# Gate angles by arc tangent and running sums, one score product a head, and a checked fallback, in a GateLoop and SwiGLU kernel

## The chip, the cores and the metric

The kernel runs on one core of a Trainium2 chip. The metric is the device time of one execution in microseconds; less is better. The core has a matrix engine (PE, with its weight loads shown apart as PEld), a vector engine (DVE), a scalar engine for activation functions (ACT), a general engine (POOL) and a queue that issues transfers (SP). Each engine takes its instructions in the order of its own queue and waits for others by semaphores.

## The reference

Four batches, eight heads, 768 steps, 48 features a head. A recurrence with complex gates, then a normalised SwiGLU feed-forward over 3,072 tokens:

```python
mag = np.sqrt(a_re * a_re + a_im * a_im)
scale = np.minimum(mag, 0.999) / (mag + 1e-06)
a_re_n, a_im_n = (a_re * scale, a_im * scale)
for t in range(S):
    new_re = ar * S_re - ai * S_im          # ar, ai: gates of step t, one for each feature d
    new_im = ar * S_im + ai * S_re
    S_re, S_im = (new_re + einsum('bhd,bhe->bhde', k[:, :, t], v[:, :, t]), new_im)
    y[:, :, t] = einsum('bhd,bhde->bhe', q[:, :, t], S_re)
x = y as (3072, 384)
xn = x / sqrt(mean(x * x) + 1e-06) * rms_g
g = xn @ w_gate                              # 384 -> 1536
out = (g * sigmoid(g) * (xn @ w_val)) @ w_out
```

The inputs: real parts of the gates are uniform between 0.85 and 0.95, imaginary parts normal with a deviation of 0.1; q, k, v normal with 0.1. The feed-forward's weights arrive as numbers of eight bytes and are made float32 on the chip. All arithmetic is float32.

## The kernel before

A gate is a magnitude times a unit phasor. The product of the phasors since the sequence's first step rotates q and k (each feature gets two rows, cosine and sine, so 96 rows a head), after which the gates are real numbers between 0 and 1. The recurrence then runs in 24 chunks of 128 steps (six for each batch), all heads together.

`gates(b, j, t)` treats 128 feature rows of a batch over all 768 steps, three times for each batch. It computes magnitudes and unit phasors (squares and a square root on ACT, a reciprocal and a Newton step on DVE, lines 103 to 126), then the running product of the phasors by `cmul` over strides 1, 4, 16, 64, 256 and back (lines 151 to 159), six DVE operations for each complex product. Cosines, sines and magnitudes go to DRAM (lines 127 and 161) and come back in the layout of the chunks in `load_unit` (lines 271 and 272).

`levels(n)` computes the weights of all pairs of steps in a chunk, without any quotient. It multiplies q and k by cosines and sines, forms the diagonal by small 32-wide products (line 295), and then goes through seven levels of halves 1, 2, ..., 64. Each level is a set of small matrix products (line 310 inside 32-step blocks, line 322 above), a masked copy or a copy into `am`, and three DVE multiplications that extend the decay factors in q, in k and in the blocks' whole products (lines 327 to 330). So one level waits for the last one's DVE work.

`finish(n)` transposes k (line 350), computes the new state (lines 354 to 361), the outputs y from `am` and v and from q and the carried state (lines 366 and 368), normalises them (ACT squares with an accumulated sum, POOL a power, ACT a scaling), transposes them on PE and scales them into `xT` (line 386).

`feed_forward(g, ffn)` runs for each group of three chunks: twelve steps f of six matrix products each (gate and val, three each; a float32 product shows as two records) with a sigmoid on ACT and two products on DVE (lines 403 to 405), then three outputs of twelve products each (line 410).

`load_weights` and `narrow` load the weights in 18 pieces of 128x768 and convert them with nine DVE operations each.

The order: the phasors of batch 0 first (lines 420 to 425), then for each chunk `step(levels(n), behind, *ahead)`, which advances the levels of the chunk, the finish of the chunk before and the phasors of the next batch in turns, with one step of the filler (weights first, then the feed-forward of the last whole group) after each round. The framework keeps priorities in that order, but puts a ready instruction into an engine's queue ahead of one that isn't expected to be ready. All transfers are issued from SP.

Of the kernel before, what the change touches and what calls it, by code (L numbers as in the profile page):

```python
"""GateLoop (a gated linear recurrence with complex gates) and then a SwiGLU feed-forward, in float32.

The recurrence S_t = a_t S_{t-1} + k_t v_t^T, y_t = q_t . Re S_t runs in chunks of 128 steps.
A gate is a magnitude times a unit phasor. The product of the phasors since the sequence's first
step rotates q and k (two rows of each feature: cosine and sine), after which the gates are real
numbers in [0, 1]. Within a chunk the weights of the pairs (t, s) with s < t come in levels of
halves 1, 2, ..., 64: a pair belongs to the one level where s lies in the lower and t in the upper
half of the same block, and its decay is (product from the upper half's start to t) times (product
after s to the lower half's end). Both are products of gates alone, without a quotient or a
logarithm, so that any gate, zero too, is treated exactly. A level is one set of matrix products  # L10
and the factors of the next level are this level's times the halves' whole products. After the
last level they are what the carried state needs.
"""
# [8 lines left out]
FP32 = mybir.dt.float32  # L22
I32 = mybir.dt.int32
U32 = mybir.dt.uint32
# [5 lines left out]
P = 128  # L30
C = 128          # steps in a chunk
BLK = 32         # steps in a diagonal block
# [3 lines left out]
SCALE = 2.0 ** 30    # gates are scaled by a power of two before they are squared  # L36
TINY = 2.0 ** -112   # squares of scaled gates below this: the gate's own value is 0 in float32
# [3 lines left out]
def gateloop_swiglu(  # L41
    ctx: ExitStack,
    tc: tile.TileContext,
    qT: bass.AP,      # [B * NCH, D, H * C]
    kT: bass.AP,      # [B * NCH, D, H * C]
    v: bass.AP,       # [B * S, H * D]
    a_re: bass.AP,    # [B, H * D, S]
    a_im: bass.AP,    # [B, H * D, S]
# [4 lines left out]
    out: bass.AP,     # [B * S, H * D]  # L53
# [12 lines left out]
    GC = 3               # chunks in a group of the feed-forward  # L66
# [12 lines left out]
    # ---------------------------------------------------------------- phasors and magnitudes  # L79
# [9 lines left out]
    def gates(b, j, t):  # L89
        """Rows j*128.. of batch b: cosine and sine of the phase up to each step, and magnitudes."""  # L90
# [18 lines left out]
        # 1 / m and 1 / (m + eps) from one reciprocal  # L109
# [5 lines left out]
        # one Newton step of r = w ** -0.5  # L115
# [4 lines left out]
        # the unit phasor (1 where the gate is 0)  # L120
# [3 lines left out]
        # min(|a|, cap) * |a| / (|a| + eps)  # L124
# [5 lines left out]
        def cmul(x, y, n):  # L130
            """y *= x for complex views (re, im) of n elements."""
# [13 lines left out]
        def view(step, g):  # L145
            """Every step-th element, in groups of g: [p, groups, g]."""
            n = S // step
            return [q.rearrange("p (n k) -> p n k", k=step)[:, :, step - 1]
                     .rearrange("p (a g) -> p a g", g=g) for q in (re, im)]
# [16 lines left out]
    # ---------------------------------------------------------------- constants  # L166
# [7 lines left out]
    # pairs of a level inside a diagonal block: steps s on the partitions, the block's upper-half  # L174
    # steps t along a row
# [15 lines left out]
    # weights of pairs, [s, head, t]: the parts before a diagonal block stay 0  # L191
# [12 lines left out]
    def load_weights(stage):  # L204
        """Weights of 4 bytes as they are; of 8 bytes, their words (low, high) made float32 here."""
# [298 lines left out]
```

## Time and profile before

| | us |
|---|---|
| median of three runs | 1414.46 (1412.72 to 1414.88) |
| span of the profiled execution | 1409.9 |
| PE busy | 997.1 (71%) |
| PEld busy | 702.6 (50%) |
| DVE busy | 1072.7 (76%) |
| ACT busy | 225.6 (16%) |
| POOL busy | 34.1 (2%) |
| mean granted PE clock | 0.896 |

A profile page describes one execution. "Busy" counts the time in which an engine has an instruction running; matmuls overlap in the pipeline, so the mean duration of one is longer than what it adds to a run of them. The granted clock is the share of full speed at which the throttle lets PE run. A line of a group gives the source line, the engine, the operation, what it writes and reads, the shape and the count, then busy time, the mean in ns of one, and the idle time of the engine just before, with who ended it. A row of a timeline gives start and duration in us.

The page's slices of the span (40, in tenths) show the stages at a glance: PE is at 0 in the first six slices while DVE is at 8 or 9, and in the last four DVE falls off while PE is full.

```profile
PE   0000005245399869986999699869997999799898
DVE  7999998998988978897899798978955642543120
```

### The profile page before, as it was taken

How to read it: one execution, taken by the hardware profiler on the slowest of the kernel's cores; microseconds unless marked ns; L12 is line 12 of the kernel's file. 1: busy time of each engine (PE TensorE's matmuls, PEld its weight loads, DVE VectorE, ACT ScalarE, POOL GpSimd, SP SyncE). 2: the span in 40 equal slices, each digit the busy share in tenths (PEclk: the TensorE clock that was granted, in tenths of full speed). 3: DMA queues.
4: the chain of work that ended last, by engine and by line, in shares of the span. 5: the costliest groups of instructions: out<-in, count | busy, mean ns of one | idle time of the engine just before them, and what ended most of it. 6: DMA issues, size and time to landing. Idle time of an engine off the chain costs nothing.

```text
span 1409.9 us, 30973 instructions
## 1 busy us (share of the span) xinstructions
PE 997.1 (71%) x13352; PEld 702.6 (50%) x13352; DVE 1072.7 (76%) x2663; ACT 225.6 (16%) x453; POOL 34.1 (2%) x54
## 2 busy tenths in 40 slices
PE   0000005245399869986999699869997999799898
PEld 0000005235266555655665666556656667666555
DVE  7999998998988978897899798978955642543120
ACT  1000001111032211211222113112111211111110
POOL 2000000000100000000000000000000000000000
PEclk9999999999999958995899599958995997699899
DMA  6223242241022222302222313021213021100000
GB/s 173 69 99 106 84 119 63 74 136 45 24 75 62 85 62 53 97 29 52 74 57 85 82 39 96 31 73 30 63 63 80 24 52 40 30 1 7 12 1 17
DMA packets 63993, 86.94 MB, mean 62 GB/s; under 512 B 5488, under 2 KB 48496, under 8 KB 63856
## 3 DMA queue, kind: packets, MB, share of 16 engines
q1 hardware_dynamic: 63856, 84.96, 21.5%
q8 instruction: 105, 1.72, 0.5%
q14 instruction: 32, 0.26, 0.1%
HBM read 66.06 MB, written 18.87 MB: 60 GB/s over the span
## 4 chain that ended last, share of the span: by engine, by line
PE 51%; DVE 39%; issue 6%; ACT 1%; DMA 1%; POOL 1%; SPq 0%; POOLq 0%; DVEq 0%; ACTq 0%
PE gate_ps L400 13%; PE val_ps L400 11%; PE out_ps L410 6%; PE s_high L322 5%; DVE k L282 4%; PE s_low L310 4%; PE y_ps L366 4%; DVE w L98 3%; DVE cs L282 3%; PE state_ps L354 3%; PE y_ps L368 3%; DVE re L98 3%; DVE mg L111 2%; DVE s L98 2%; DVE m L98 2%
## 5 line engine op out<-in xcount | busy, mean ns | idle before, releaser
L400 PE MATMUL gate_ps<-xT,wg 128*128 128x384 f32 x576 | 231.7, 539 | 0.7 <-DVE xT L386 0.7
L400 PE MATMUL val_ps<-xT,wv 128*128 128x384 f32 x576 | 205.2, 492 | 0.0
L410 PE MATMUL out_ps<-wo,hT 128*128 128x384 f32 x576 | 192.0, 490 | 0.0
L295 PE MATMUL s_diag<-q,k 96*32 96x32 f32 x1536 | 23.4, 228 | 218.2 <-DVE k L282 214.4
L310 PE MATMUL s_low<-cs,k 96*32 96x16 f32 x7680 | 111.0, 199 | 86.0 <-DVE k L282 77.0
L310 PEld LDWEIGHTS s_low<-cs,k 96*32 96x32 f32 x7680 | 97.8, 131 | 131.2 <-issue 65.8
L400 PEld LDWEIGHTS val_ps<-xT,wv 128*128 128x128 f32 x576 | 110.9, 194 | 79.7 <-issue 5.7
L400 PEld LDWEIGHTS gate_ps<-xT,wg 128*128 128x128 f32 x576 | 113.1, 209 | 64.5 <-issue 13.8
L410 PEld LDWEIGHTS out_ps<-wo,hT 128*128 128x128 f32 x576 | 107.7, 190 | 71.3
L282 DVE TENSOR_TENSOR cs<-cs,bp 96x512 f32<-96x512 f32 x144 | 98.6, 685 | 49.9 <-PE s_high L322 49.7
L295 PEld LDWEIGHTS s_diag<-q,k 96*32 96x32 f32 x1536 | 20.4, 140 | 223.5 <-DVE k L282 214.4
L322 PE MATMUL s_high<-cs,k 96*32 96x32 f32 (+1 forms) x1152 | 79.2, 237 | 68.8 <-DVE k L282 47.4
L322 PEld LDWEIGHTS s_high<-cs,k 96*32 96x32 f32 (+1 forms) x1152 | 70.1, 150 | 88.7 <-issue 70.0
L404 DVE TENSOR_TENSOR sg<-gate_ps,sg 128x384 f32<-128x384 f32 x96 | 52.8, 550 | 63.7 <-ACT sg L403 63.4
L282 DVE TENSOR_TENSOR k<-k,bp 96x512 f32<-96x512 f32 x144 | 97.8, 679 | 0.0
L403 ACT ACTIVATE sg<-gate_ps 128x384 f32<-128x384 f32 x96 | 47.0, 489 | 276.2 <-PE gate_ps L400 263.0
L366 PE MATMUL y_ps<-v,amat 128*128 128x48 f32 x384 | 89.2, 334 | 0.7 <-ACT amat L324 0.7
L368 PE MATMUL y_ps<-state,cs 96*128 96x48 f32 x320 | 80.0, 340 | 0.0
L366 PEld LDWEIGHTS y_ps<-v,amat 128*128 128x128 f32 x384 | 75.2, 249 | 2.4 <-ACT amat L324 0.8
L405 DVE TENSOR_TENSOR hT<-val_ps,sg 128x384 f32<-128x384 f32 x96 | 53.1, 553 | 29.7 <-PE val_ps L400 29.6
L313 DVE COPY_PREDICATED dg<-pairs,s_low 128x128 f32<-128x128 int32 x120 | 41.3, 344 | 43.6 <-PE s_low L310 41.9
L368 PEld LDWEIGHTS y_ps<-state,cs 96*128 96x128 f32 x320 | 66.8, 258 | 0.0
(82 smaller groups left out, 1316.1 us busy)
## 6 DMA issues: line engine op xcount, KB each, us to landing
q<-in_q_dram SPq DMA_DIRECT2D x48, 192.0 KB, 3.4
k<-in_k_dram SPq DMA_DIRECT2D x48, 192.0 KB, 3.6
mg<-mag SPq DMA_DIRECT2D x48, 192.0 KB, 4.1
re<-in_a_re_dram SPq DMA_DIRECT2D x12, 384.0 KB, 3.2
im<-in_a_im_dram SPq DMA_DIRECT2D x12, 384.0 KB, 4.0
v<-in_v_dram SPq DMA_DIRECT2D x24, 192.0 KB, 2.6
raw<-in_w_gate_dram SPq DMA_DIRECT2D x6, 768.0 KB, 4.8
mag<-mg SPq DMA_DIRECT2D x12, 384.0 KB, 2.5
```

What stands on the lines that cost most here:

```text
L98: nc.vector.tensor_tensor(out=o, in0=x, in1=y, op=op)
L282: tt = lambda o, x, y: nc.vector.tensor_tensor(out=o, in0=x, in1=y, op=ALU.mult)
L295: nc.tensor.matmul(ps[bs, h], lhsT=k[:, h, bs], rhs=q[:, h, bs], start=True, stop=True)
L310: nc.tensor.matmul(ps[bs, h].rearrange("s (j r) -> s j r", r=m), lhsT=k[:, h, bs], rhs=rhs, start=True, stop=True)
L322: nc.tensor.matmul(ps[lo, h], lhsT=k[:, h, lo], rhs=qd[:, h, hi], start=True, stop=True)
L366: nc.tensor.matmul(ps[:, h], lhsT=am[:, h], rhs=vv[:, h], start=True, stop=prev is None)
L368: nc.tensor.matmul(ps[:, h], lhsT=qd[:, h], rhs=prev[:, h], start=False, stop=True)
L400: nc.tensor.matmul(p_, lhsT=w_[:, d, fs], rhs=xT[:, d], start=d == 0, stop=d == ND - 1)
L403: nc.scalar.activation(out=sg, in_=gp, func=AF.Sigmoid)
L404: nc.vector.tensor_tensor(out=sg, in0=gp, in1=sg, op=ALU.mult)
L405: nc.vector.tensor_tensor(out=hT[:, f], in0=vp, in1=sg, op=ALU.mult)
L410: nc.tensor.matmul(ps, lhsT=hT[:, f, i * C:(i + 1) * C], rhs=wo[:, f], start=f == 0, stop=f == NF - 1)
```

## The change

The old kernel function stays, renamed `general`, with its comments removed. A new function `fast` computes the same result in another way, and a new `gateloop_swiglu` calls `fast`, reads a flag that `fast` left and runs `general` behind it, in a conditional block, if the flag is above 0.

In `fast`:

- The gates are treated in units of two chunks (12 units), in a layout of 128 rows by 3 x 256 for all heads of the batch. The angle is the arc tangent of im / re; the running angle is a sum (a scan), reduced to one turn by rounding, and its cosine and sine come from the sine function. The magnitude's running product within a chunk is a scan too. q is multiplied by that product and k by its reciprocal, so that one plain matrix product for each head gives all the pairs' weights of a chunk; a causal mask finishes them.
- Rotated q and k are rearranged by transfers inside SBUF from the gates' layout to the 96-row layout; DRAM is no longer passed. The decay over a chunk goes the same way in four-byte rows.
- The state is computed as (state products + old state) x decay.
- ACT's Silu takes the place of the sigmoid and one DVE product.
- Conversion of the weights takes one ACT square and six DVE operations a piece, and the pieces are pulled by the first group's feed-forward, two before every second f.
- Each output of the feed-forward has a second pause in its middle, so a group has 18 filler steps; the loop runs one filler step after each part of the scores and two after each part of the finish.
- The flag counts entries outside the range in which the shortcuts hold: decays of a chunk not between 2^-40 and 1, or real parts outside 2^-7 to 2^7.

The core of the diff (lines of `general` that only lost comments are left out):

```diff
+PI = 3.14159265358979
+ROUND = 1.5 * 2.0 ** 23
+RE_MIN = 2.0 ** -7
+RE_MAX = 2.0 ** 7
+P_MIN = 2.0 ** -40
...
-def gateloop_swiglu(
+def general(
...
+def fast(tc, ctx, qT, kT, v, a_re, a_im, w_gate, w_val, w_out, rms_g, out, H, bad):
...
+    def load_gates(u):
+        b, c = divmod(u * UC, NCH)
+        t = UN[u]
+        for name, ap in (("re", a_re), ("im", a_im)):
+            t[name] = prep.tile([P, ND, T], FP32, tag=name, name=name, bufs=2)
+            rows = ap[b].rearrange("(h j l) s -> j l h s", j=ND, l=L)
+            for j in range(ND):
+                nc.sync.dma_start(out=t[name][:, j], in_=rows[j][:, :, c * C:c * C + T])
...
+    def gates(u):
+        t = UN[u]
+        re, im, q, k = (t[x] for x in ("re", "im", "q", "k"))
+        act_ = nc.scalar.activation
+
+        s, w, y, r, p, ks, qs = (prep.tile([P, ND, T], FP32, tag=x, name=x)
+                                 for x in ("s", "w", "y", "r", "p", "ks", "qs"))
+        act_(out=s, in_=re, func=AF.Square)
+        act_(out=w, in_=im, func=AF.Square)
+        tt(s, s, w, ALU.add)
+        act_(out=y, in_=re, func=AF.Abs_reciprocal_sqrt)
+        act_(out=y, in_=y, func=AF.Square)
+        act_(out=r, in_=s, func=AF.Abs_reciprocal_sqrt)
+        act_(out=w, in_=re, func=AF.Abs, bias=mid)
+        act_(out=w, in_=w, func=AF.Relu, bias=width, accum_out=range_[:, u:u + 1])
+
+        tt(im, im, y)
+        tt(re, re, y)
+        stt(im, re, 2.0, im, ALU.subtract, reverse0=True)
+        yield
+
+        tt(w, s, r)
+        stt(s, w, -0.5, r, ALU.mult)
+        stt(w, s, 1.5, w, ALU.add)
+
+        act_(out=r, in_=r, func=AF.Identity, scale=-CAP * EPS_MAG, bias=cap)
+        stt(w, w, EPS_MAG, r, ALU.subtract, ALU.min)
...
+        nc.vector.tensor_tensor_scan(out=flat(p), data0=flat(w),
+                                     data1=starts.rearrange("p j c t -> p (j c t)"),
+                                     initial=0.0, op0=ALU.mult, op1=ALU.add)
+        nc.vector.tensor_copy(out=ends[:, u], in_=p.rearrange("p j (c t) -> p j c t", t=C)[:, :, :, C - 1])
+        yield
+        act_(out=r, in_=p, func=AF.Abs_reciprocal_sqrt)
+        act_(out=r, in_=r, func=AF.Square)
+        act_(out=im, in_=im, func=AF.Arctan)
+        act_(out=im, in_=im, func=AF.Copy, scale=0.5 / PI)
+
+        tt(s, p, r)
+        stt(r, s, 2.0, r, ALU.subtract, reverse0=True)
+        tt(k, k, r)
+        tt(q, q, p)
+        yield
+
+        for j in range(ND):
+            nc.vector.tensor_tensor_scan(
+                out=re[:, j], data0=im[:, j], data1=zeros, op0=ALU.add, op1=ALU.add,
+                initial=UN[u - 1]["turn"][:, j] if u * UC % NCH else 0.0)
+        act_(out=w, in_=re, func=AF.Identity, bias=round_)
+        stt(im, w, ROUND, re, ALU.subtract, ALU.add, reverse0=True)
+        turn = t["turn"] = prep.tile([P, ND, 1], FP32, tag="turn", name="turn", bufs=2)
+        nc.vector.tensor_copy(out=turn, in_=im[:, :, T - 1:T])
+        act_(out=w, in_=im, func=AF.Abs)
+        act_(out=s, in_=im, func=AF.Sin, scale=2 * PI)
+        act_(out=y, in_=w, func=AF.Sin, scale=-2 * PI, bias=halfpi)
+        yield
+        tt(ks, k, s)
+        tt(k, k, y)
+        tt(qs, q, s)
+        tt(q, q, y)
+        rot = {"kc": k, "ks": ks, "qc": q, "qs": qs}
+        yield
+        for i in range(UC):
+            n = u * UC + i
+            for name in ("k", "q"):
+                to = U[n][name] = unit.tile([D2, H, C], FP32, tag=name, name=name, bufs=3)
+                for a, part in enumerate("cs"):
+                    for j in range(ND):
+                        nc.sync.dma_start(
+                            out=to[a * D + j * L:a * D + (j + 1) * L],
+                            in_=rot[name + part][:, j, i * C:(i + 1) * C])
...
+        nc.scalar.activation(out=to, in_=as_to(hi.bitcast(FP32)), func=AF.Square)
+        stt(as_to(g.bitcast(FP32)), to, (1.125 * 2.0 ** -15) ** 2, as_to(hi.bitcast(FP32)), ALU.is_ge)
...
+    def scores(n):
...
+        for a in range(2):
+            ps = ps_a.tile([C, hh, C], FP32, tag="a", name="s_ps")
+            for h in range(hh):
+                nc.tensor.matmul(ps[:, h], lhsT=k[:, a * hh + h], rhs=q[:, a * hh + h],
+                                 start=True, stop=True)
+            nc.vector.tensor_tensor(out=am[:, a * hh:(a + 1) * hh], in0=ps, op=ALU.mult,
+                                    in1=causal.unsqueeze(1).to_broadcast([C, hh, C]))
+        yield
...
+    def feed_forward(g, pieces):
...
+            if f * P % FW == 0:
+                next(pieces, None)
+                next(pieces, None)
...
+            nc.scalar.activation(out=sg, in_=gp, func=AF.Silu)
+            tt(hT[:, f], vp, sg)
+            yield
...
+                if f == NF // 2:
+                    yield
...
+    load_gates(1)
+    for _ in gates(0):
+        pass
...
+    def run(x, fill):
+        for _ in x:
+            for _ in range(fill):
+                next(filler, None)
+            next(ahead, None)
+
+    behind = None
+    for n in range(N + 1):
+        if n % UC == 0 and n // UC + 1 < NU:
+            for _ in ahead:
+                pass
+            if n // UC + 2 < NU:
+                load_gates(n // UC + 2)
+            ahead = gates(n // UC + 1)
...
+        if n < N:
+            run(scores(n), 1)
+        if n > 0:
+            run(finish(n - 1), 2)
+        if n % GC == 0 and n:
+            for _ in filler:
+                pass
+            filler = feed_forward(n // GC - 1, pieces)
...
+def gateloop_swiglu(tc, qT, kT, v, a_re, a_im, w_gate, w_val, w_out, rms_g, out, H):
+    nc = tc.nc
+    with tc.tile_pool(name="flag", bufs=1) as flag:
+        bad = flag.tile([1, 1], I32, name="bad")
+        with ExitStack() as ctx:
+            fast(tc, ctx, qT, kT, v, a_re, a_im, w_gate, w_val, w_out, rms_g, out, H, bad)
+        with tc.If(nc.values_load(bad[0:1, 0:1]) > 0):
+            general(tc, qT, kT, v, a_re, a_im, w_gate, w_val, w_out, rms_g, out, H)
```

216 lines of the change are left out of this document (added).

## The prediction

> **What bounds the kernel now.** I read the page's chain of work first, then the waits, then a cut of the span into stretches. In the page's part 4 (share of the span by engine) and in the view of the waits (total, times, longest) these lines carry it; the four rows of the windows view give a stretch, its length, then the busy time of PE, of weight load (PEld), of DVE, ACT, POOL with counts, the granted clock and the DMA share:
>
> ```profile
> PE 51%; DVE 39%; issue 6%; ACT 1%; DMA 1%; POOL 1%; SPq 0%; POOLq 0%; DVEq 0%; ACTq 0%
> PE s_diag L295 <- DVE k L282: 214.4, 1, 214.4
> 0.00:214.00 214.00, 0.00 (x0) 0.00 (x0) 206.13 (x510) 12.36 (x14) 9.54 (x30) 1.00 0.36 108
> 214.00:391.00 177.00, 78.27 (x2034) 72.16 (x2034) 163.90 (x414) 22.18 (x49) 10.44 (x3) 1.00 0.25 70
> 391.00:1334.00 943.00, 847.29 (x11105) 588.65 (x11104) 688.77 (x1715) 183.69 (x376) 14.14 (x21) 0.85 0.20 54
> 1334.00:1410.00 76.00, 71.53 (x217) 41.76 (x216) 13.93 (x25) 7.32 (x15) 0.00 (x0) 0.97 0.02 8
> ```
>
> There are four stages with different limits. For 214 us PE has no record at all: DVE computes the phasors of batch 0 in 206 us of its time, and the first score product waits for it. To 391 us DVE is still 93% busy (164 of 177) and PE 44%. Then PE and DVE take turns as the bound, at a mean granted clock of 0.85. The last 76 us are the feed-forward of the last group, PE alone.
>
> **What PE's work costs.** A matmul's shown duration contains its latency, so I take start-to-start distances in the timeline (start, duration), where PE runs without a gap at full clock:
>
> ```profile
> 1340.23 2.10 PE L400 MATMUL gate_ps<-xT,wg 128*128 128x384 f32 x6
> 1342.16 2.10 PE L400 MATMUL val_ps<-xT,wv 128*128 128x384 f32 x6
> 1344.10 2.10 PE L400 MATMUL gate_ps<-xT,wg 128*128 128x384 f32 x6
> 1382.80 23.38 PE L410 MATMUL out_ps<-wo,hT 128*128 128x384 f32 x72
> 824.65 0.55 PE L385 MATMUL xT_ps<-ident,xn 128*128 128x128 f32 x3
> 825.03 2.10 PE L400 MATMUL gate_ps<-xT,wg 128*128 128x384 f32 x6
> 859.57 0.88 PE L350 MATMUL kt_ps<-ident,k 96*128 96x96 f32 x8
> 860.38 0.36 PE L310 MATMUL s_low<-cs,k 96*32 96x16 f32 x18
> 860.69 1.56 PE L354 MATMUL state_ps<-v,kt 128*96 128x48 f32 x16
> 862.09 2.17 PE L400 MATMUL gate_ps<-xT,wg 128*128 128x384 f32 x6
> 866.63 0.42 PE L366 MATMUL y_ps<-v,amat 128*128 128x48 f32 x2
> ...
> 870.28 2.25 PE L400 MATMUL gate_ps<-xT,wg 128*128 128x384 f32 x3
> ```
>
> One f of the feed-forward is 1344.10 - 1340.23 = 3.87 us, so 12 are 46.4; the three outputs are about 23.3. A group is **69.7 us**, eight are 558. The change leaves these products alone. Of a chunk, kt is 0.81, state 1.40, y 3.65 and xT 0.38 us; these stay too. kt, state and half of y are missing in one chunk of six, or so little fewer that I take 5.5 us a chunk for them together.
>
> **The change, term by term.**
>
> *Scores.* The levels go (64 s_diag, 320 s_low and 48 s_high records a chunk, with the DVE work between them). In their place stand 8 heads x 2 records with 128 weight columns and 128 moving ones. The trace has no such pair in float32. y, 32 records in 3.65 us, has 128 weight columns and 48 moving ones: 0.114 us each, set by the weights. If the 128 moving columns (384 take 3.87 / 12 = 0.32, so 0.107) lie beside the load, a chunk costs 16 x 0.114 = 1.8 us; if behind it, 16 x 0.22 = 3.5. I take 1.9, since y shows loads beside the stream. So attention is **7.4 us a chunk**.
>
> *The clock.* Low-stream work drops the clock:
>
> ```profile
> 684.00:732.00 48.00, 48.00 (x552) 30.91 (x551) 43.38 (x87) 12.06 (x24) 0.55 (x1) 1.00 0.14 39
> 732.00:744.00 12.00, 12.00 (x160) 8.62 (x159) 9.95 (x74) 1.83 (x5) 0.55 (x1) 0.86 0.21 50
> 744.00:774.00 30.00, 30.00 (x279) 17.74 (x279) 29.93 (x49) 6.66 (x11) 0.00 (x0) 1.00 0.28 94
> ```
>
> PE is busy throughout and still gets 0.86 in the 12 us with a y: 1.7 us lost. In the new order state and y stand together (5 us of narrow products), so I take 2.2 us for each chunk, from 0 to 4.
>
> *DVE.* The gates of a unit of two chunks become 17 tensor operations on 128x768, one scan of 768 and three of 256, and a few tiny ones. Back to back, 768 elements take the distance of the first two rows here; the others give 512 from PSUM or SBUF, 384, a one-source operation, and the slowest of this width:
>
> ```profile
> 704.32 0.95 DVE L98 TENSOR_TENSOR mg<-m,mg 128x768 f32<-128x768 f32 x1
> 705.19 0.95 DVE L98 TENSOR_TENSOR w<-w,r 128x768 f32<-128x768 f32 x1
> L282 DVE TENSOR_TENSOR cs<-cs,bp 96x512 f32<-96x512 f32 x144 | 98.6, 685 | 49.9 <-PE s_high L322 49.7
> L405 DVE TENSOR_TENSOR hT<-val_ps,sg 128x384 f32<-128x384 f32 x96 | 53.1, 553 | 29.7 <-PE val_ps L400 29.6
> L236 DVE TENSOR_SCALAR t<-raw 128x768 int32<-128x768 int32 x18 | 9.8, 547 | 0.0
> L111 DVE RECIPROCAL mg<-mg 128x768 f32<-128x768 f32 x12 | 59.3, 4943 | 0.0
> ```
>
> 17 x 0.87 = 14.8 us. No scan is in this trace: 1,536 elements cost 1.8 us at the rate of a tensor_tensor and 9.9 at the reciprocal's; I take 1.8, the nearer kind, and 1 us for the tiny ones: 17.6 a unit. Two chunks add 4 masks (0.69), 4 state operations, 2 xT (0.55 each) and 8 products hT: about 2.7 + 3.3 + 4.4 = 10.4. So **28 us of DVE in each 66 us of PE** (two chunks, 14.8, with 12 of 18 filler steps, 46.5, and the dips, 4.4). The long scan costs up to 8 us more without becoming the bound. [...]
>
> *ACT.*
>
> ```profile
> L103 ACT ACTIVATE s<-re 128x768 f32<-128x768 f32 x12 | 10.1, 842 | 210.4 <-DVE re L98 208.7 <-DMA re<-in_a_re_dram 1.6
> L108 ACT ACT_TABLE_LOAD x8 | 10.3, 1283 | 4.7 <-DVE w L98 4.5
> L403 ACT ACTIVATE sg<-gate_ps 128x384 f32<-128x384 f32 x96 | 47.0, 489 | 276.2 <-PE gate_ps L400 263.0
> L351 ACT COPY kt<-kt_ps 128x384 f32<-128x384 f32 x40 | 18.2, 479 | 42.8 <-PE kt_ps L350 42.7
> ```
>
> 16 activations of 768 a unit are 13.5 us, and the four kinds (inverse root, arc tangent, sine, silu) alternate: 5 to 7 table loads of 1.28, some 8 us. With silu 8 x 0.49, kt, x, xn and two ot about 5.5, ACT has 31 of 66 us. A late silu is covered: four PSUM buffers let PE run two f ahead (7.7 us). If that cover goes, every load costs 1.28 us on the path, 100 us in 11 units at seven. [...]
>
> *DMA.* Now the angles cross DRAM; then q and k are rearranged inside SBUF by 24 transfers of 128 rows of 512 B a unit, plus 12 of four-byte rows for the decays, plus 10 loads.
>
> ```profile
> q1 hardware_dynamic: 63856, 84.96, 21.5%
> cs<-sin SPq DMA_DIRECT2D x24, 192.0 KB, 4.5
> 859.67 0.81 SPq L262 DMA_DIRECT2D q<-in_q_dram  x2
> ```
>
> I count some 96,000 packets, 1.5 times as many, in two thirds of the time: under 50% of the engines. SP issues 50 transfers a unit at 0.4 us, 20 of 66. Behind a waiting rearrangement on SP stand the next loads and the out stores; the last of the gates' six steps is issued while some 20 us of PE work for the older chunk is left, against 5 us of issue and 4.5 of landing. Hidden; without the cover 10 us a unit.
>
> *The start.* DVE and ACT alternate through gates(0). The first activation is at 3.70; 15 dependent DVE steps (13), 14 ACT steps (12) and three table loads (4) give some 32 us alone. But 18 pieces of weights must be converted (three float scalar-tensor operations, a tensor_tensor, two one-source ones: 4 x 0.87 + 2 x 0.47 = 4.4 us each, 79 in all), and this program order lets such work slip in between dependent steps:
>
> ```profile
> 3.70 0.84 ACT L103 ACTIVATE s<-re 128x768 f32<-128x768 f32 x1 [1.61 <-DMA re<-in_a_re_dram]
> 20.61 0.95 DVE L98 TENSOR_TENSOR w<-w,r 128x768 f32<-128x768 f32 x1
> 21.48 0.56 DVE L236 TENSOR_SCALAR t<-raw 128x768 int32<-128x768 int32 x1
> 21.94 0.95 DVE L98 TENSOR_TENSOR w<-w,r 128x768 f32<-128x768 f32 x1
> 1406.77 0.33 SPq L415 DMA_DIRECT2D out_dram<-ot  x1
> ```
>
> A step then comes every 1.33 us in place of 0.87, so I take 45 us a chain. gates(1) reuses the single buffers of gates(0), so chunk 2 has q and k at about 4 + 2 x 45 + 9 = 103, and its mask, y, norm and xT (10 us, PE at half clock) put the first feed-forward product at **113** (95 to 130). From there PE has work: 558 + the scores of chunks 4 to 23 and the ends of 3 to 23, 20.5 x 7.4 (152) + 20 dips x 2.2 (44) = 754. To that I add 15 us for the first group, whose weights are still being converted (by its end DVE owes 3.5 units of gates, 79 of conversion, six chunks and 12 hT, 165 us), and 3% for handovers, 19. The end: the last row above is 3.1 us before the span's 1409.9; the read of the flag and the jump over the old code are not in this trace, 0 to 9 us (two landings of 4.5), I take 5. 113 + 754 + 15 + 19 + 3 + 5 = 909 of span. The execution profiled, 1409.9, lies 4.6 under the median 1414.46, so **914**, rounded to 915, against 1414.46.
>
> **Rivals.**
>
> (a) *The chain of handovers sets the pace.* A unit's gates need about 30 changes between DVE and ACT, each behind whatever stands in those queues; prep's single buffers let only one unit be in work. At 45 us it fits in 66; at 80 the ten later units cost 10 x 14 = 140 more: 1055. For it: 1.33 us steps above; against it: DVE and ACT under half busy. Chance 0.17.
>
> (b) *The clock.* If the narrow products hold the clock at 0.80 for the whole of PE's 710 us, 178 are lost in place of 44: 1050. For it: 0.85 over 943 us before; against it: much of that was idle PE. 0.08.
>
> (c) *ACT's table loads reach PE.* As priced, 7 x 1.28 x 11 = 99 us: 1015; by the measured rows no cover is lost, and 0.05. [...]
>
> (d) *All hides better*: no dip beyond that now seen, start at 95, scores 1.8: 915 - 44 - 18 - 15 = about 840. 0.08.
>
> (e) *Slower than before.* The fallback is taken: the flag exceeds 0 if one decay of 128 steps is below 2^-40 or above 1, or one real part leaves 2^-7 to 2^7. Then the whole old program runs behind the new: 915 + 1405 = 2320. The inputs speak against it: real parts 0.85 to 0.95, magnitudes about 0.9, 0.9^128 is about 2^-19; it takes a table result that is off or not a number. 0.04. That the change then does not do what it says is this same case.
>
> **How the numbers follow.** Forecast 0.57, (a) 0.17, (b) 0.08, (c) 0.05, (d) 0.08, (e) 0.04, and 0.01 that unseen things eat all of it. A range of 840 to 1060 leaves out (e), the last, and the tails of the others, below 0.2. A measurement of this kernel tells about 0.2% from no change; only (e) and the 0.01 are not faster: faster 0.95, same 0.01, slower 0.04.
>
> **What would show it.** The first gate product near 113 us and PE without gaps from about 200 on; DVE and ACT under half busy there; 66 us between the gates of one unit and the next; scores at about 1.9 us a chunk; clock dips after each y. Wrong would be: PE waiting on DVE's k or q in every unit (a), a clock under 0.85 in the middle (b), gate products released by silu (c), or a span beyond 2000 (e).

## The result, and the profile after

The changed kernel takes 933.95 us (median of four runs, 931.5 to 935.99), against 1413.59 of the kernel before beside it (1411.12 to 1414.88). The ratio is 0.661, with a 95% interval from 0.6593 to 0.6626. The forecast was 915, with a range from 840 to 1060. The profiled execution of the changed kernel took 935.99, the slowest of the four; its span is 934.3. Of all the runs below only two, of experiment 9 (911.25 and 916.17 us), count as slow, with a lower granted clock than the others of their kernel.

The page of the changed kernel, its slices of the span and its chain of work:

```profile
PE   0134885388688899999999999999999999999997
...
DVE  5896454797797364362554622735612101110110
...
PEclk9998575688797999898999999999999999899999
...
q1 hardware_dynamic: 105520, 61.46, 24.1%
...
PE 76%; DVE 10%; ACT 3%; issue 2%; DMA 1%; POOL 0%; DVEq 0%; ACTq 0%; SPq 0%
```

DVE's share of the chain has gone from 39% to 10%, and PE's slices are full from the fifteenth on. In front of that stand fourteen slices, a third of the span, where PE isn't full and its clock (PEclk) sinks to half. The windows view, cut at the first score product, at the first feed-forward product and at the point from which PE has no gap any more:

```profile
0.00:43.50 43.50, 0.00 (x0) 0.00 (x0) 29.52 (x39) 28.39 (x33) 2.27 (x17) 1.00 0.60 170
43.50:125.70 82.20, 47.04 (x233) 45.11 (x233) 52.98 (x77) 42.12 (x59) 1.65 (x3) 0.75 0.30 79
125.70:315.20 189.50, 138.37 (x563) 93.98 (x564) 141.38 (x202) 86.25 (x116) 3.54 (x5) 0.79 0.38 104
315.20:926.00 610.80, 610.80 (x2569) 403.99 (x2568) 206.60 (x327) 213.45 (x323) 9.61 (x16) 0.97 0.17 46
```

The fourth row is what the change was to reach: PE busy for all of 610.8 us, DVE and ACT for a third of it. The third row is the weak place. The first feed-forward group and its five chunks need some 110 us of PE (73.6 for the group and one step f of the next, five chunks at 7.2) and take 189.5: PE has no record for 51 of them, and the mean clock of the stretch is 0.79. The view of the waits, for the whole span, names who ended PE's gaps (total, times, longest; two rows of the start and of the norm left out):

```profile
PE val_ps L776 <- DVE wv L501: 24.2, 4, 12.0
...
PE state_ps L728 <- DVE am L707: 22.8, 4, 12.5
...
PE s_ps L705 <- DVE am L707: 12.9, 1, 12.9
...
PE out_ps L787 <- DVE wo L501: 7.2, 3, 3.3
```

Two kinds of wait are to be explained: for converted weights (`wv`, `wo`, 31 us) and for masks (`am`, 36 us). The norm's, 15 us, is smaller and isn't followed here. The timeline (start, duration) follows one of each, and then shows some rows of the dense stretch and the last copy; many rows are left out between these:

```profile
65.85 1.91 SPq L619 DMA_DIRECT2D k<-k  x3
...
77.94 3.62 PE L705 MATMUL s_ps<-q,k 96*128 96x128 f32 x16
...
94.03 1.28 DVE L707 TENSOR_TENSOR am<-s_ps,causal 128x512 f32<-128x512 f32 x2
...
109.87 1.90 SPq L619 DMA_DIRECT2D k<-k  x3
...
125.77 2.92 PE L776 MATMUL gate_ps<-xT,wg 128*128 128x384 f32 x4 [0.65 <-DVE xT L759]
...
140.84 0.49 SPq L656 DMA_DIRECT2D raw<-in_w_val_dram  x1
...
148.06 2.80 PE L728 MATMUL state_ps<-v,kt 128*96 128x48 f32 x16 [8.20 <-DVE am L707]
...
163.68 1.48 PE L728 MATMUL state_ps<-v,kt 128*96 128x48 f32 x16
...
175.24 0.87 ACT L662 ACTIVATE wv<-raw 128x768 f32<-128x768 f32 x1
...
185.04 4.21 PE L776 MATMUL val_ps<-xT,wv 128*128 128x384 f32 x6 [12.04 <-DVE wv L501]
...
371.16 0.39 PE L739 MATMUL y_ps<-v,am 128*128 128x48 f32 x2
...
371.63 0.63 PE L739 MATMUL y_ps<-v,am 128*128 128x48 f32 x2
...
392.15 1.95 PE L705 MATMUL s_ps<-q,k 96*128 96x128 f32 x16
393.94 2.10 PE L776 MATMUL gate_ps<-xT,wg 128*128 128x384 f32 x6
...
397.81 0.82 PE L716 MATMUL kt_ps<-ident,k 96*128 96x96 f32 x8
...
928.38 0.48 ACT L792 COPY ot<-out_ps 128x384 f32<-128x384 f32 x1 [7.31 <-PE out_ps L787]
```

The fourth piece of weights leaves SP only at 140.84, 15 us after the first feed-forward product. Ahead of it SP issues the rearrangement of two units, from 65.85 and from 109.87 on, at 0.63 us a transfer (three in 1.91), with decays and loads behind each. In the 75 us from 65.85 to 140.84 it issues for 62; for the other 13 (97.1 to 109.9) it stands, with the second rearrangement waiting for its data and the load of weights behind it. The piece is squared at 175.24, behind two chunks' work and gates in ACT's order, and PE has it at 185. The masks of chunk 2: its score products end at 81.5, the mask comes at 94.03, and the first feed-forward product 32 us behind that.

### The profile page after: what moved, and what is told of

Read it like the earlier page. It is cut to its first block, busy times and chain, and to the rows that moved or that the text cites. A ratio compares the mean times of both kernels' runs of the same rounds, so it can differ in the third digit from the quotient of the medians.

```text
span 934.3 us, 9261 instructions
## 1 busy us (share of the span) xinstructions
PE 798.5 (85%) x3370; PEld 544.1 (58%) x3370; DVE 430.5 (46%) x641; ACT 370.7 (40%) x530; POOL 17.1 (2%) x41
## 2 busy tenths in 40 slices
DMA packets 105574, 62.14 MB, mean 67 GB/s; under 512 B 28720, under 2 KB 99376, under 8 KB 105520
## 3 DMA queue, kind: packets, MB, share of 16 engines
q1 hardware_dynamic: 105520, 61.46, 24.1%
## 4 chain that ended last, share of the span: by engine, by line
PE 76%; DVE 10%; ACT 3%; issue 2%; DMA 1%; POOL 0%; DVEq 0%; ACTq 0%; SPq 0%
PE out_ps L787 20%; PE gate_ps L776 20%; PE val_ps L776 18%; PE y_ps L739 5%; PE y_ps L741 4%; PE s_ps L705 3%; PE state_ps L728 3%; PE kt_ps L716 1%; PE xT_ps L758 1%; DVE t L504 1%; DVE g L504 1%; DVE w L504 1%; DVE im L504 1%; DVE p L579 1%; DMA raw<-in_w_gate_dram 1%
## 5 line engine op out<-in xcount | busy, mean ns | idle before, releaser
L705 PE MATMUL s_ps<-q,k 96*128 96x128 f32 x384 | 55.5, 305 | 56.5 <-DMA k<-k 43.6
L705 PEld LDWEIGHTS s_ps<-q,k 96*128 96x128 f32 x384 | 54.6, 220 | 62.5 <-issue 44.0
L739 PE MATMUL y_ps<-v,am 128*128 128x48 f32 x384 | 78.9, 303 | 0.0
L741 PE MATMUL y_ps<-state,q 96*128 96x48 f32 x320 | 70.5, 306 | 0.0
L739 PEld LDWEIGHTS y_ps<-v,am 128*128 128x128 f32 x384 | 65.6, 221 | 0.8
L741 PEld LDWEIGHTS y_ps<-state,q 96*128 96x128 f32 x320 | 57.1, 222 | 0.0
L728 PE MATMUL state_ps<-v,kt 128*96 128x48 f32 x320 | 34.9, 269 | 22.8 <-DVE am L707 22.8
L728 PEld LDWEIGHTS state_ps<-v,kt 128*96 128x96 f32 x320 | 34.6, 187 | 27.5 <-DVE am L707 23.7
L707 DVE TENSOR_TENSOR am<-s_ps,causal 128x512 f32<-128x512 f32 x48 | 32.5, 687 | 39.2 <-PE s_ps L705 39.1
L717 ACT COPY kt<-kt_ps 128x384 f32<-128x384 f32 x40 | 17.3, 478 | 46.6 <-PE kt_ps L716 46.6
```

The lines of the kernel that those rows point to most:

```text
L705: nc.tensor.matmul(ps[:, h], lhsT=k[:, a * hh + h], rhs=q[:, a * hh + h], start=True, stop=True)
L707: nc.vector.tensor_tensor(out=am[:, a * hh:(a + 1) * hh], in0=ps, op=ALU.mult, in1=causal.unsqueeze(1).to_broadcast([C, hh, C]))
L717: nc.scalar.copy(out=kt[:, a * hh:(a + 1) * hh], in_=ps)
L728: nc.tensor.matmul(ps[:, h], lhsT=u["kt"][:, h], rhs=vv[:, h], start=True, stop=True)
L739: nc.tensor.matmul(ps[:, h], lhsT=am[:, h], rhs=vv[:, h], start=True, stop=prev is None)
L741: nc.tensor.matmul(ps[:, h], lhsT=q[:, h], rhs=prev[:, h], start=False, stop=True)
```

## The experiments

Each stands alone on the changed kernel, if nothing else is said. Times are medians, the ratio is that to the kernel before with its 95% interval; the changed kernel has 0.661.

**1. Weights in another queue.** Theory A: in the first group the loads of the weights are late because they stand in SP's queue behind the rearrangement. Theory B: DVE, with 79 us of conversion, is too slow.

```diff
-        nc.sync.dma_start(out=raw, in_=src)
+        nc.gpsimd.dma_start(out=raw, in_=src)
```

> Only the queue of the 18 raw weight loads is changed, from SP to POOL's own. In the changed kernel the first group's products run from 125.8 to 315.2 us, 190 us for about 95 us of PE work, and between 60 and 175 us no piece of the weights is converted, though DVE is busy for only 53 of the 82 us from 43.5 to 125.7. Theory A (the loads stand behind rearrangement transfers in SP's queue): the next pieces are converted from 60 us on, and the first group ends some 60 us earlier, total 870 to 890. Theory B (DVE's throughput bounds the stretch): nothing moves, 930 to 937. Theory C (priority: the loads come early but the DVE operations still stand behind gates and chunks in the order): 915 to 937, with the raw tiles full and waiting.

Measured: 888.65 us (886.38 to 892.39), 0.6286 (0.6266 to 0.6307). The windows of this run, cut at its first feed-forward product:

```profile
0.00:154.40 154.40, 47.35 (x233) 45.44 (x233) 119.87 (x165) 79.06 (x101) 14.85 (x33) 0.82 0.50 142
154.40:250.00 95.60, 93.46 (x406) 63.20 (x407) 79.59 (x115) 51.76 (x72) 6.69 (x8) 0.95 0.37 107
```

Its waits:

```profile
PE state_ps L728 <- DVE am L707: 41.3, 4, 14.2
...
PE out_ps L787 <- DVE wo L501: 0.2, 1, 0.2
```

From the first feed-forward product to the end it takes 733 us (887.4 - 154.4) in place of 808.5, so 75 less, and the wait for weights is gone. But that first product comes 29 later: DVE is now busy 120 of the first 154 us, and the masks wait for it. So 45 remain of the 75. With not one DVE operation less the kernel gains them, which B can't give; the time lies in A's range.

**2. Conversion earlier.** The same loads, still in SP's queue, but pulled by the first four chunks instead of by the first group.

```diff
-    filler = iter(())
+    filler = pieces
```

> Only the place of the conversion in the program order is changed: the pieces are the filler of chunks 0 to 3, before the first feed-forward. Theory A (SP's queue): loads move ahead too, so the first group shortens, 860 to 900. Theory B (DVE throughput): what the first group gains, the first chunks lose, 925 to 940. Theory C (priority): 860 to 890, first feed-forward product later than 125.8 us by 10 to 30 us, but without waits for wv afterwards.

Measured: 900.08 us (899.45 to 906.82), 0.6368 (0.6357 to 0.6379). The longest wait of PE behind its start:

```profile
PE s_ps L705 <- DMA decay<-ends: 26.3, 1, 26.3
```

A score product now waits 26 us for a decay's transfer, which SP issues too. One queue carries both, and whichever is put ahead makes the other late. The first feed-forward product comes at 141.9, 16 later, and no wait for `wv` is left, as theory C had it; the time lies at the edge of A's range and above C's. So this run doesn't tell A from C; experiment 1 does.

**3. No conversion.** The six DVE operations of each piece are left out.

> Leaves out the six DVE operations of each of the 18 pieces; ACT's square of the high words stands in the weights' place, loads and ACT work stay. All theories expect a gain. A: loads still come late (about 140 us), first group ends near 240, total 860 to 880. B: 79 us of DVE go, total 855 to 870. It bounds what any reordering of the conversion can bring.

Measured: 902.27 us (901.61 to 902.93, two runs), 0.638 (0.6368 to 0.6393). The fourth piece of weights, as SP issues it in this run (one of the last for val follows at 212.79):

```profile
138.44 0.49 SPq L656 DMA_DIRECT2D raw<-in_w_val_dram  x1
```

That is above both ranges, so the expectation missed. 79 us of DVE work less bring 32, fewer than the other queue with all of that work. The loads stay late without it. So DVE's time counts in this stretch, but it isn't the first limit.

**4. More DVE work.** Four extra products of 128x768 a unit, each about 0.87 us.

```diff
-        tt(ks, k, s)
+        for _ in range(3):
+            tt(ks, k, s)
...
-        tt(qs, q, s)
+        for _ in range(3):
+            tt(qs, q, s)
```

> Four more DVE multiplications of 128x768 in each unit (the two sine products are computed three times over), 3.5 us of DVE a unit, 42 us in all; outputs as before. If DVE bounds the first 315 us (B), the four to five units treated there cost 14 to 18 us, 948 to 953, and the rest nothing. If order bounds it (A or C), 934 to 942: only the two gate chains ahead of the first products grow, by 3.5 us each. If DVE mattered in the dense part too, it would be 976.

Measured: 946.37 us (941.38 to 954.3), 0.668 (0.6658 to 0.6703), 12 more. The first feed-forward product moves from 125.8 to 131.8. From 330 to 900 PE still has no gap:

```profile
330.00:900.00 570.00, 570.00 (x2421) 379.66 (x2420) 225.95 (x343) 202.14 (x308) 10.46 (x16) 0.96 0.18 48
```

DVE does 24 us more than the changed kernel in this stretch (201.5 there), beside PE. What remains of the cost is in the first 330 us and in one hundredth of clock (5.7 us). The median lies between the ranges, 942 and 948, and the profiled run is the slowest of the four, so this run doesn't decide between B and order; it shows that DVE costs little behind the first 330 us.

**5. Scores twice.** Is PE the limit behind the first group, and what does a score product cost?

```diff
-            for h in range(hh):
+            for h in list(range(hh)) * 2:
```

> Every score product is issued twice (the second writes the same numbers); nothing else changes. Theory that PE sets the pace from the first feed-forward product on: the second set costs its own 1.79 us a chunk, 15 scores in the dense stretch = 27 us and up to 9 more before it = 43: 961 to 977 us, and PE without a gap in the dense stretch. Rival that handovers between the engines set the pace there: the second set lies in PE's waits, 934 to 940. Rival that a second 128-column product costs more than the 1.79 (load not beside the stream, 3.5 a chunk): 987 or more.

Measured: 951.66 us (948.76 to 954.33), 0.6733 (0.6712 to 0.6753): 18 more, below the first theory's 27 to 43 and above the rival's 0 to 6. Two rows of its timeline:

```profile
380.78 3.74 PE L705 MATMUL s_ps<-q,k 96*128 96x128 f32 x32
384.35 2.10 PE L776 MATMUL gate_ps<-xT,wg 128*128 128x384 f32 x6
```

384.35 - 380.78 = 3.57, twice the 1.79 of the changed kernel (393.94 - 392.15). So a set costs its full price where PE is busy. From the end of the first group to the end of the span it takes 646.5 us (951.2 - 304.7) in place of 619.1 (934.3 - 315.2): 27.4 more for the 15 scores there, as the first theory had it. The total is less because the first group ends 10.5 us earlier, and PE's idle time shrinks by 10. The expectation had missed that; what made the start shorter isn't shown.

**6. The state's products apart from y's.** One feed-forward step stands between them now.

```diff
             U[n + 1]["state"] = new
+        yield
...
-            run(scores(n), 1)
+            run(scores(n), (1, 1))
...
-            run(finish(n - 1), 2)
+            run(finish(n - 1), (2, 1, 1))
```

> One feed-forward step is put between the state's products and y's, so that the narrow products no longer stand together; the number of filler steps a chunk stays 6. Theory that the clock's dips come from 5 us of narrow products in a row: the dense stretch gets back up to its 18 us of dips, 916 to 930. Rival that y alone (3.6 us) is enough for a dip: 930 to 940, and the same granted clock in the stretch from 330 to 900.

Measured: 919.13 us (918.8 to 922.54), 0.6513 (0.6497 to 0.6529), 15 less. The stretch from 330 to 900, first in the changed kernel:

```profile
330.00:900.00 570.00, 570.00 (x2442) 379.93 (x2441) 201.53 (x320) 204.02 (x311) 9.61 (x16) 0.97 0.17 45
```

and in this run:

```profile
330.00:900.00 570.00, 570.00 (x2474) 379.53 (x2473) 197.38 (x312) 190.02 (x297) 8.76 (x16) 0.99 0.16 43
```

The granted clock goes from 0.97 to 0.99, and PE gets 32 more records done in the same 570 us. Cut into pieces of 6 us, the clock's loss over this stretch is 17 us in the changed kernel and 7 here. So 10 of the 15 are dips, and the time is what the theory forecast. That it takes 5 us in a row isn't shown, though. In the changed kernel a y without state products ahead of it, from 463.80 to 467.43, has a dip behind it too:

```profile
468.00:474.00 6.00, 6.00 (x16) 3.36 (x15) 4.92 (x9) 4.06 (x8) 0.55 (x1) 0.79 0.24 67
```

Two of the three such y's in its dense stretch have one, so y alone can be enough. Nor is the size sure. Between 330 and 870 the same count gives 8 to 24 us in the nine versions with state and y together, and 3 to 7 in the three with a step between them (experiments 6, 10 and 12). One more version with both together, that of experiment 8, has a mean clock of 0.99 from 330 to 900 all the same.

**7. No branch.** The read of the flag, the block and the old algorithm are left out.

> The read of the flag, the conditional block and the old algorithm in it are left out; the flag itself is still computed. The prediction had 5 us for this read and jump. From the trace, where the last store ends some 3 us before the span does: 931 to 934. Rival: the old program's code delays the start (loading of code) or the end, 925 or less.

Measured: 925.53 us (919.61 to 927.88), 0.6545 (0.6516 to 0.6575), 8 less. The last copy of this run, whose span is 922.8:

```profile
919.45 0.48 ACT L792 COPY ot<-out_ps 128x384 f32<-128x384 f32 x1 [7.31 <-PE out_ps L787]
```

From the end of the last copy to the end of the span it is 2.9 us here (922.8 - 919.93) and 5.4 in the changed kernel (934.3 - 928.86). So the flag and the jump cost 2.5 us where they stand. The other 6 lie ahead of the last copy, so the median is nearer to the rival's 925 than to 931 to 934. The first feed-forward product comes 3 earlier (122.8), and some 5 are the clock (0.98 from 330 to 900, in place of 0.97). Other versions differ by as much in both, so it isn't shown that code that isn't run delays anything; that stays open.

**8. The branch taken.** The comparison lets the block be entered always (`> -1`).

> The comparison lets the block be entered always, so the old algorithm runs behind the new one and writes the same output again. By the prediction's last rival: 934 + 1405 = about 2340. If code that is reached by a jump has to be fetched first, some 5 to 20 us more; if the new part had hidden costs of the old one (buffers, loads), less.

Measured: 2328.3 us in one run, 12 below the expectation's 2340. The prediction's case (e) had 2320: the price of the fallback is about the sum of both kernels, and no more. The 5 to 20 us for fetching code were the author's guess, and no run shows them.

**9. The third unit's gates later.** Theory C: the first feed-forward product is late because the mask of chunk 2 stands in DVE's queue behind the gates of the third unit.

```diff
             for _ in range(fill):
                 next(filler, None)
-            next(ahead, None)
+            if n not in (2, 3):
+                next(ahead, None)
...
             for _ in ahead:
-                pass
+                next(filler, None)
```

> The gates of the third unit are not advanced during chunks 2 and 3 (until chunk 2 is finished), and are then interleaved with the first feed-forward steps. Theory that the mask of chunk 2 (scores done at 81.5, first gate product 44 us later) stands in DVE's queue behind the gates of the third unit, which wait for ACT: the first gate product comes at 95 to 108 in place of 125.8. Theory that the end of the first group is set by the weights' loads in SP's queue: little of it arrives at the end, 925 to 936; if the start alone counted, 910 to 916. Rival for the start (PE's half clock and the chain from y to xT): first gate product at 118 to 126.

Measured: 907.34 us (897.14 to 916.17), 0.6441 (0.6398 to 0.6485). The timeline:

```profile
77.02 3.62 PE L705 MATMUL s_ps<-q,k 96*128 96x128 f32 x16
...
93.11 1.28 DVE L707 TENSOR_TENSOR am<-s_ps,causal 128x512 f32<-128x512 f32 x2
...
96.05 0.49 SPq L656 DMA_DIRECT2D raw<-in_w_val_dram  x1
...
123.03 3.57 PE L776 MATMUL gate_ps<-xT,wg 128*128 128x384 f32 x5 [0.65 <-DVE xT L759]
```

A miss in its purpose, and a gain by another way. The framework put the same gates ahead of the mask again, since their data was there, and the first product stays at 123. But their rearrangement now comes later, so the fourth piece of weights leaves SP at 96 in place of 140.8: theory A once more. The gain is 27 us by the median, and 34 by its runs of 897.14 and 903.43, more than any theory gave. Not all of it is the weights: in the profiled run PE's waits for them fall from 33 to 24 us, those for masks from 36 to 28, and the clock's loss between 330 and 870 from 17 to 8.

**10. Three edits together:** experiments 1, 6 and 9.

> Three edits together: the weights' loads in POOL's queue, the third unit's gates later, one feed-forward step between state and y. If the three are limits of their own: the first group without waits for weights (45 us, as in the first experiment), some 10 of dips, and the first gate product at 100 to 130 in place of 154: 850 to 875. Rival that DVE's work on weights and gates in the first 300 us is then the bound: 875 to 890, with the first gate product at 140 or later or PE waiting for DVE in the first group.

Measured: **882.28 us** (879.46 to 882.61), 0.6244 (0.6229 to 0.6259), the best version of all. It fell in the rival's range: the first feed-forward product stays at 154.7, and PE waits 40.4 us for masks.

**11. The gates behind the masks.** As in 9, and the third and fourth unit's inputs are loaded only ahead of chunk 3's scores, so that the framework can't move their gates up.

```diff
-            if n // UC + 2 < NU:
+            if n // UC + 2 < NU and n > 2:
                 load_gates(n // UC + 2)
...
+        if n == 3:
+            load_gates(2)
+            load_gates(3)
```

> As the run with the gates later, but the third unit's loads are issued only ahead of chunk 3's scores, so that on DVE its gates now stand behind the masks of chunks 2 and 3 (in the last run the framework had put them ahead again, and DVE's rows between 77 and 93 were the same). Theory that the masks behind these gates hold the first gate product: s_ps of chunk 2 is done at 81, its mask comes at 82 in place of 93, and the first gate product at 100 to 112 in place of 123; 885 to 900 us if the weights follow, 900 to 910 if they are then late again. Rival (PE at half clock with y at 7 us a chunk, and the chain of norm and transposition): first gate product still at 118 to 125.

Measured: 904.53 us (896.49 to 908.94), 0.6398 (0.6357 to 0.6439). The timeline of this run:

```profile
75.74 3.56 PE L705 MATMUL s_ps<-q,k 96*128 96x128 f32 x16
...
77.69 0.69 DVE L707 TENSOR_TENSOR am<-s_ps,causal 128x512 f32<-128x512 f32 x1 [1.15 <-PE s_ps L705]
...
106.23 3.97 PE L776 MATMUL gate_ps<-xT,wg 128*128 128x384 f32 x6 [0.65 <-DVE xT L759]
```

Its waits for weights:

```profile
PE val_ps L776 <- DVE wv L501: 19.7, 4, 6.6
...
PE gate_ps L776 <- DVE wg L501: 11.0, 3, 5.7
```

Theory C of experiment 9 holds: the mask comes at 77.7, and the first feed-forward product at 106.2, 17 us earlier than in 9. The kernel gains nothing measurable by it over 9, since PE then waits 31 us for weights.

**12. One buffer for raw weights.** The edits of 10 and 11, and one buffer in place of two, which was to spread the loads.

> As the run with three edits (882), with the loads of the third and fourth unit issued ahead of chunk 3's scores as in the last run, and with one buffer for the raw weights in place of two. Theory that in POOL's queue the loads run so far ahead that DVE converts 12 of the 18 pieces (53 us of it) before the first feed-forward product, and so delays the gates of chunk 2 and the masks: with one buffer a load can start only when the piece before is converted, the conversions spread out, and the first gate product comes at 115 to 138 in place of 154; 855 to 874 us. Rival that the pieces then come too late for the first group: PE waits for wg, wv or wo 10 us and more, 878 to 895. Rival that it is the gates themselves that DVE does first: first gate product at 145 or later, 875 to 885.

Measured: 905.81 us (901.52 to 909.85), 0.6425 (0.64 to 0.645), worse than 10 and above all three ranges. The signs of both rivals came in: the first feed-forward product at 150.5, and the loads too late. PE's wait for the last weights:

```profile
PE out_ps L788 <- DVE wo L501: 15.3, 4, 6.5
```

The last load in POOL's queue, in the timeline:

```profile
263.97 0.72 POOL L656 DMA_DIRECT2D raw<-in_w_out_dram  x1 [13.01 <-DVE ssq L747]
```

PE waits for masks 35.5 us besides. With nothing of the weights in SP's queue, the third unit's inputs arrive early again, and its gates stand ahead of chunk 2's masks as in 9. An order that has both the early start of 11 and the weights of 10 wasn't found within these runs.

## Why the prediction came near, point by point

That it came so near is in part luck: errors of opposite sign nearly cancel. The forecast's span was 909, the measured one 934.3. By its steps:

- **The first group (15 us for weights still being converted): the step that failed.** With its five chunks at 7.4 + 2.2 the forecast allows 110 + 15 + 11 = 136 us for the third row of the windows, which took 189.5: 54 more. The prediction priced SP's transfers at 0.4 us, from two loads of q (0.81), and called the queue hidden, "20 of 66". A transfer of the rearrangement takes 0.63, and at the start two units' worth stand ahead of the weights. The prediction had named what stands behind a waiting rearrangement ("the next loads and the out stores") but not these loads, and put the weights down to DVE. Experiment 1 takes 75 us out between the first feed-forward product and the end by the queue alone, and 45 net, since that product comes 29 later; 2, 3 and 9 agree. The 189.5 are 110 of work, 51 of waits, 33 of them for weights, and 28 by which PE is slower; for the last two the forecast had 15 and 11. How much of the waits for weights is SP's lateness itself and how much the place that a late load then gets in ACT's order (from its issue at 140.84 to its square at 175.24) wasn't told apart.
- **The start (113): 12.8 too early, with a wrong course.** The chains of gates are faster than the 45 us taken: chunk 2's scores start at 77.94, where its q and k were expected at 103. From there to the feed-forward the forecast had 10 us, and it takes 48. Experiment 11 shows some 17 of them to be masks behind another unit's gates. And in the second row of the windows the products themselves cost nearly double: a chunk's scores take 3.62 us at 77.94 against 1.95 at 392.15. The granted clock there shows this only in part: it reads 1.00 between 78 and 81.4, and 0.50 from 97.4 to 103.7, where y takes 0.43 us for a pair, as behind 371.63.
- **The rest: 36 less.** From 315.2 to 928.4 are 613 us: 484 of feed-forward (seven groups less that one f), 18 of dips (610.8 x 0.03), and the 111 that are left for the attention of 15 to 16 chunks, 7.2 each. Handovers (19, which is not quite 3% of 754) cost nothing: PE has no gap from 315 to the last copy. For the dips 16 chunks at 2.2 had been taken, 35. A dip costs about that, 2.4 us, but only 7 of the 16 y's show one, where the prediction expected one after each. What picks them isn't shown.
- **The end: 2 less.** 934.3 - 928.4 = 5.9, where 3 + 5 had been taken; the flag's part is 2.5 (experiment 7). With 54 + 13 - 36 - 2 = 29 and 4 less by attention at about 7.2 us a chunk in place of 7.4, 909 becomes 934.
- **Terms that held.** A step f is 3.87 us still (397.81 - 393.94). The scores of a chunk are 1.79, taken at 1.9. ACT is busy 213 of the 611 us, DVE 207. The gates of a unit come every 62 us (five steps between the last two rows below), with 66 forecast.
- **DMA** takes 24.1% of the engines with 105,520 packets, "under 50%" with some 96,000 forecast. In the third row of the windows their share is 38%: there the queue that issues was the limit, not the engines.

Three rows of the view by lines (count, then busy time and mean in ns):

```profile
L579 DVE TENSOR_TENSOR_SCAN p<-w,starts 128x768 f32<-128x768 f32 x12 | 20.8, 1734 | 0.0
...
L596 DVE TENSOR_TENSOR_SCAN re<-im,turn,zeros 128x256 f32<-128x256 f32 x24 | 17.5, 741 | 0.6 <-ACT im L587 0.6
...
L779 ACT ACT_TABLE_LOAD x27 | 34.6, 1283 | 0.5
```

The first and the last of the six long scans in the dense stretch, in the timeline:

```profile
344.19 1.73 DVE L579 TENSOR_TENSOR_SCAN p<-w,starts 128x768 f32<-128x768 f32 x1
...
654.95 1.73 DVE L579 TENSOR_TENSOR_SCAN p<-w,starts 128x768 f32<-128x768 f32 x1
```

- **Scans** were taken at 1.8 us a unit and take 1.73 + 3 x 0.74 = 3.9. The rate of a tensor_tensor, which had been taken, is too fast for them: in this trace the long scan takes 1.73 us, and a tensor_tensor of this width 0.95. The 2 us a unit cost nothing in the dense stretch, where PE has no gap beside them.
- **The rivals.** (a) Handovers don't set the pace: no gap, 62 us a unit. (b) The clock is 0.97 in the dense stretch, not 0.80; it is 0.75 and 0.79 in the two stretches where PE waits. (c) No wait of PE for silu shows between 315 and 926, with 27 table loads ahead of silu in the whole span at 1.28 us. Each costs ACT about its own length here: the load at 68.36 follows an activation that ends at 68.35, and the next one starts 1.30 us behind the load's start. Of (d) the scores came in (1.79), and about half of its gain on dips; its start and its first group didn't. (e) didn't occur; its price is as worked out.

## What to carry to other kernels

Count a queue's issue time where it stands, not as a share of a steady stage: 36 small transfers of 0.63 us held a load behind them for 23 us here, though the DMA engines were busy for only 0.33 of that stretch (65.85 to 140.84), and a rearrangement that waited for its data held it for 13 more. At a start, where nothing covers, list for each engine and queue what stands ahead of the first thing that the bound engine needs; a framework that takes ready work first puts the next unit's work there. Narrow products in a row can cost more than their time, here 0.43 us for a pair in y in place of 0.22; with a wide product between them the clock of the dense stretch was 0.99 in all three versions that have it, and 0.96 to 0.98 in the others but one (experiment 8, 0.99 in its single run).

## What wasn't expected of the hardware

- In the dense stretch of the changed kernel the clock halves for a while in or behind 7 of the 16 y's, though PE has no gap: in the y of the rows above a pair of records takes 0.22 us up to 371.16 and 0.43 from 371.63 on (0.63 in place of 0.39 for a pair's own duration), and the granted clock is 0.50 from 371.63 to 377. With one step of feed-forward between state and y 7 of 17 us of this are left.
- Where PE waits it is also slower when it works: the state's products take 2.80 us at 148.06, behind a wait of 8.2 and at a granted clock of 0.50, and 1.48 at 163.68 with no wait ahead of them and at 1.00. The granted clock is 0.75 and 0.79 in the second and third row of the windows, against 0.97 in the fourth, and early in the span it reads 1.00 where the products are already slow. In the third row 28 us by which PE is slower stand beside 51 of waits, so a microsecond of waiting there went with more than one lost.
- POOL issues a load of weights in 0.72 to 0.91 us (experiments 1 and 12; 0.72 in the last row of 12), SP in 0.37 to 0.54 in the changed kernel. It is the dearer queue, and the better one here (45 us less in experiment 1), since no rearrangement is issued from it.
